# Aligned SBUF tiles, other buffer counts and a new order of the first batch's loads in a fused attention and mixer kernel

## The chip, the cores and the metric

The kernel runs on one core of a Trainium2 chip, in one launch. The metric is the time of an execution on the device in microseconds; a profiled execution also has a span, from the first to the last instruction that the profiler records. TensorE (PE) multiplies matrices, with its weight loads recorded apart (PEld); VectorE (DVE) and ScalarE (ACT) work elementwise, GpSimd (POOL) makes small copies and issues the loads from HBM, and SyncE (SP) issues the transposing DMAs and the stores. Each engine works through its own list of instructions in order.

## What is computed

Eight batches go through a gated attention without softmax and then through a mixer with two multilayer parts. Cut to what matters:

```python
batch, seq, d_model, d_qk = 8, 3008, 256, 64            # d_tok 256, d_ch 1536
scores = (1.0 / seq) * np.matmul(z, z.transpose(0, 2, 1))
attn   = np.maximum(scores, 0.0) ** 2
x      = u * np.matmul(attn, v)                          # the gate
h      = np.maximum(x.transpose(0, 2, 1) @ w_tok1, 0.0) @ w_tok2
y      = x + h.transpose(0, 2, 1)
out    = y + np.maximum(y @ w_ch1, 0.0) @ w_ch2          # float32
```

Queries and keys are the same z, so the scores are symmetric: the block of query block q and key block g is the transpose of the block of g and q.

## The kernel before

**Tiles.** The 3008 rows of a batch are cut into six blocks of 512 (the last has 448 rows, and its last 64 stand twice, in both halves of the partitions). A block of queries q meets six blocks of keys g. For each pair, one score-square tile `at` of 128 x 2048 bf16 is made: four score matmuls (line 379) with 64 rows of contraction, two at a time on the two halves of the array, write PSUM; ACT applies relu (417, or 405 on the diagonal); DVE squares in place (425, 453). Then eight matmuls (line 513, "av") multiply it with the tile of v, four for each half of the 256 columns, into the accumulators `acc0` and `acc1`. After six key blocks DVE multiplies the accumulators with the transposed u, `uT` (gate, line 606), and a transposing DMA on SP turns the result `xT` into `x_sb` (618). In this text six av blocks make a query block, and 36 av blocks, called steps, a batch.

**Mirrors.** Where symmetry is used, a tile `at` of block (q, g), g > q, is also turned by a transposing DMA on SP (`flip`, line 472) into a tile `fl`, the mirror, which serves block (g, q) later without scores, relu or square. Lines 224 to 227 say which blocks are made directly: all of batch 0, the upper half and the diagonal of each later batch, and in batch 1 also those with g = 0. On the diagonal of later batches only a triangle of scores is made and the rest is filled by transposes (465). Ten buffers hold mirrors, six hold `at`.

**Mixer.** When the last query block of a batch is done, its mixer is added to a list of pieces that PE runs between the av blocks of the next batch: `tok1` (653), `tok2` (670), `ch1` (707) and `ch2` (748). ch1's result `hp` is evacuated with relu by ACT (720) or DVE (722) into `h2` tiles (eight buffers); ch2's result `op` gets the residual on DVE (760, 775), and SP stores it (764, 778). Batch 7's mixer runs alone at the end.

**Order.** The order of every engine's instructions is written out beforehand by a planner in the kernel's own Python (lines 961 to 1045). It keeps clocks for PE, ACT, DVE and SP with due times for each kind of operation (`push(engine, ready, busy, lat, ...)`), and room counters (`live`, `ROOM`) for the buffers, and picks at each point a run of up to three pairs of scores, an av half or a mixer piece. Its times are constants; on the chip the engines wait for semaphores. Stretches of scores use half the array's rows, and PE's order changes between the two kinds of matmul 282 times.

**Loads.** `at_group(n, f)` (line 885) makes f be called when step n begins, so that its instructions go to the end of POOL's and SP's lists there. POOL's list is served in order: a load whose buffer is still in use, or a copy whose input has not landed, holds everything behind it. In batch 0 POOL carries the following. `load_v` of the batch's own six tiles at the start (line 149, from a pool of eight buffers that all batches share); `load_u` (160, two buffers; freed when `turn_u` has transposed the tile), two steps after each query block begins and two blocks ahead; w_tok1 (178), w_tok2 (189) and w_ch (208, 213) in turns from step 5 or 8 on; `order_w_tok2` (199, 203), which rewrites the loaded w_tok2 from its single staging buffer `ws` and so waits for that load; z of the next batch (99) from step 18 on, with a doubling copy for each (111) that waits for the load and for one of two buffers; and from step 28 on the six tiles of v of batch 1.

```python
at_group(base + (NQ - 1) * NG - 2 + (j if j > 1 else 0),
         lambda b=b, c=c: load_v(b + 1, c))
```

The lines that the change and the steps touch: 76 to 80 and 866 (constants and the small tile `mark`), 147, 158, 187 and 860 (pools of v, u, ws), 227, 270 (ROOM), 442, 614 and 701 (due times on SP), 735 to 783 (ch2 and its residual), 807 (needs of ch2), 901 to 907 and 930 to 942 (steps of the loads).

## Time and profile before

| what | value |
|---|---|
| 13 runs, median (lowest to highest) | 1175.47 us (1172.24 to 1186.24) |
| the profiled execution's own time | 1179.05 us |
| its span | 1177.2 us |
| mean granted TensorE clock | 0.998 |
| DVE, ACT, POOL busy | 47%, 44%, 14% of the span |
| HBM read, written | 65.40 MB, 24.64 MB: 76 GB/s |
| DMA packets | 462339, of them 426224 under 512 B |

The profiled execution took 3.58 us longer than the median of the runs, and 1.85 us of its time lie outside of the span. PE is busy nearly throughout, so the time is read from where PE is not busy or runs slowly, and from the number of its matmuls. A matmul record is longer than its turn on PE, since matmuls overlap; the pace is read from a run of them: 12 matmuls of 512 columns take 2.59 us on the chain that ended last, 0.216 us each. In the timeline, the bracket behind a row gives the idle time of the engine before it and what ended it.

### The profile page before, as it was taken

The numbers are of one execution on the slowest core, as the hardware profiler recorded it, in microseconds if no ns is written. First come the engines' busy times: TensorE is split into PE (matmuls) and PEld (weight loads), VectorE is DVE, ScalarE is ACT, GpSimd is POOL, SyncE is SP. The second block draws the span as 40 slices with busy tenths as digits, with TensorE's granted clock in tenths as the row PEclk, the third lists the DMA queues.
The fourth block names the chain that finished last, engine by engine and source line by source line (L and its number), as shares of the span: only waits on it lengthen the run. The fifth ranks groups of instructions, "written<-read, shape, count | busy, mean of one in ns | idle before, by whom it ended". The sixth has DMA issues, their size and how long they took to land.

```text
span 1177.2 us, 17741 instructions
## 1 busy us (share of the span) xinstructions
PE 1157.2 (98%) x6971; PEld 630.8 (54%) x7069; DVE 556.8 (47%) x836; ACT 523.5 (44%) x652; POOL 161.8 (14%) x328
## 2 busy tenths in 40 slices
PE   8998999999999999999999999999999999999998
PEld 3334455555546555465555655556455564555666
DVE  5774755445433554335534356342653337411544
ACT  7886544425533355433544345243553434433221
POOL 2372200101111010110201101012010110000000
PEclk9999999999999999999999999999999999999999
DMA  8999956998779987887959888699778989651232
GB/s 146 135 133 167 162 113 128 167 152 146 141 139 168 159 148 131 157 161 142 157 118 182 152 161 142 119 179 161 133 136 145 182 133 165 116 124 37 58 77 68
DMA packets 462339, 162.95 MB, mean 138 GB/s; under 512 B 426224, under 2 KB 439856, under 8 KB 462256
## 3 DMA queue, kind: packets, MB, share of 16 engines
q1 hardware_dynamic: 434400, 129.12, 60.1%
q0 software_dynamic: 27344, 32.32, 19.7%
q8 instruction: 55, 0.90, 0.3%
q10 hardware_dynamic: 512, 0.38, 0.1%
q14 instruction: 28, 0.23, 0.1%
HBM read 65.40 MB, written 24.64 MB: 76 GB/s over the span
## 4 chain that ended last, share of the span: by engine, by line
PE 90%; DMA 6%; POOL 2%; issue 1%; DVE 1%; ACT 0%; SPq 0%; POOLq 0%; DVEq 0%
PE acc L513 36%; PE op L748 21%; PE hp L707 21%; PE sc L379 5%; PE a_ps L653 4%; PE h_ps L670 3%; DMA ws<-in_moe_w_tok_dram 2%; DMA zT<-zr 1%; DMA ur<-in_u_dram 1%; DMA v_sb<-in_v_dram 1%; DMA uT<-ur 1%; POOL w_tok_sb L199 1%; DMA zf<-in_z_dram 1%; POOL v_sb L149 0%; POOL zr L111 0%
## 5 line engine op out<-in xcount | busy, mean ns | idle before, releaser
L417 ACT ACTIVATE at<-sc 128x1024 bf16<-128x1024 f32 (+1 forms) x294 | 281.0, 1023 | 212.2 <-PE sc L379 207.6
L513 PE MATMUL acc<-at,v_sb 128*128 128x512 bf16 (+2 forms) x1471 | 355.7, 379 | 8.9 <-DMA v_sb<-in_v_dram 5.7
L513 PEld LDWEIGHTS <-v_sb 128*128 128x128 bf16 (+1 forms) x2304 | 209.6, 98 | 275.4 <-issue 67.6
L720 ACT ACTIVATE h2pre<-hp 128x1024 bf16<-128x1024 f32 (+1 forms) x183 | 183.5, 1007 | 303.0 <-PE hp L707 300.3
L425 DVE TENSOR_TENSOR at<-at 128x1024 bf16<-128x1024 bf16 (+1 forms) x294 | 205.1, 705 | 178.2 <-ACT at L417 177.0
L707 PE MATMUL hp<-xT,w_ch_sb 128*128 128x512 bf16 (+1 forms) x1120 | 262.9, 374 | 1.6
L748 PE MATMUL op<-w_ch_sb,h2pre 128*128 128x256 bf16 x2208 | 258.4, 273 | 0.4 <-DVE xT L676 0.2
L748 PEld LDWEIGHTS <-h2pre 128*128 128x128 bf16 x2208 | 215.9, 98 | 46.2 <-issue 0.5
L513 PE MATMUL acc<-fl,v_sb 128*128 128x512 bf16 (+1 forms) x775 | 186.8, 370 | 1.9 <-issue 0.8
L707 PEld LDWEIGHTS <-w_ch_sb 128*128 128x128 bf16 x1152 | 112.7, 98 | 126.7
L760 DVE TENSOR_TENSOR res<-op,u_sb 128x512 f32<-128x512 f32 x88 | 60.9, 692 | 209.2 <-PE op L748 206.1
L722 DVE TENSOR_SCALAR h2pre<-hp 128x1024 bf16<-128x1024 f32 (+1 forms) x105 | 126.6, 1206 | 54.4 <-PE hp L707 53.3
L606 DVE TENSOR_TENSOR xT<-acc,uT 128x512 bf16<-128x512 f32 (+1 forms) x96 | 63.3, 665 | 109.0 <-PE acc L513 108.7
L405 ACT ACTIVATE at<-sc 128x512 bf16<-128x512 f32 (+3 forms) x164 | 59.3, 447 | 87.5 <-PE sc L379 75.8
L379 PE MATMUL sc<-zT 64*128 64x512 bf16 (+1 forms) x752 | 97.8, 360 | 0.3
L453 DVE TENSOR_TENSOR at<-at 128x512 bf16<-128x512 bf16 (+3 forms) x164 | 46.8, 338 | 47.9 <-ACT at L405 47.9
L111 POOL COPY zr<-zs 128x512 bf16<-128x512 bf16 x42 | 27.1, 646 | 294.0 <-DMA zT<-zr 293.5
L379 PEld LDWEIGHTS <-zT 64*128 64x128 bf16 x752 | 32.0, 94 | 57.8 <-issue 40.0
L160 POOL DMA_DIRECT2D ur<-in_u_dram x48 | 25.9, 541 | 236.6 <-DMA uT<-ur 234.4
L676 DVE TENSOR_TENSOR xT<-xT,h_ps 128x1024 bf16<-128x1024 bf16 (+1 forms) x48 | 55.6, 1192 | 5.5 <-PE h_ps L670 5.5
L670 PE MATMUL h_ps<-w_tok_sb,a_sb 128*128 128x512 bf16 (+1 forms) x184 | 43.9, 374 | 0.5
L149 POOL DMA_DIRECT2D v_sb<-in_v_dram x48 | 26.0, 546 | 134.1 <-PE acc L513 133.9
(43 smaller groups left out, 229.3 us busy)
## 6 DMA issues: line engine op xcount, KB each, us to landing
out_dram<-res SPq DMA_DIRECT2D x88, 256.0 KB, 2.4
v_sb<-in_v_dram POOLq DMA_DIRECT2D x40, 256.0 KB, 5.3
ur<-in_u_dram POOLq DMA_DIRECT2D x40, 256.0 KB, 5.5
zs<-in_z_dram POOLq DMA_DIRECT2D x35, 64.0 KB, 4.6
at<-at SPq DMA_TRANSPOSE x123, 2.6
fl<-at SPq DMA_TRANSPOSE x100, 4.5
v_sb<-in_v_dram POOLq DMA_DIRECT2D x8, 192.0 KB, 6.7
w_ch_sb<-in_moe_w_ch_dram POOLq DMA_DIRECT2D x4, 384.0 KB, 7.1
```

Of the source, the lines that this page charges most:

```text
L379: nc.tensor.matmul(sc[:, r, c0:c1], zT[h, k * P:(k + 1) * P], zT[h, q * QW + c0:q * QW + c1], start=True, stop=True)
L405: nc.scalar.activation(a3[:, i, c0:c1], sc[:, r, c0:c1], ACT.Relu, scale=inv_S)
L417: nc.scalar.activation(view, sv, ACT.Relu, scale=inv_S)
L425: nc.vector.tensor_mul(view, view, view)
L513: nc.tensor.matmul(o, vs[blk.b, g][rows, i, dh * P:(dh + 1) * P], rhs, start=first, stop=stop, skip_group_check=True)
L606: nc.vector.tensor_mul(xT[:, dh, :full * P].rearrange("p (t s) -> p t s", s=P), acc[:, :full * P].rearrange("p (t s) -> p t s", s=P), uT[: ...
L670: nc.tensor.matmul(h[:, dh, :W], st["a"][:, th, dh * P:(dh + 1) * P], w_tok2_sb[:, th, q * QW:q * QW + W], start=(th == 0), stop=(th == 1))
L707: nc.tensor.matmul(hp[:, r, :W], w_ch1_sb[:, dc, cc * P:(cc + 1) * P], xT[:, dc, :W], start=(dc == 0), stop=(dc == DT - 1))
L720: nc.scalar.activation(h2[:, :, :W], hp[:, :, :W], ACT.Relu)
L722: nc.vector.tensor_single_scalar(h2[:, :, :W], hp[:, :, :W], 0.0, AX.max)
L748: nc.tensor.matmul(op[:, i, :], h2, w_ch2_sb[:, cc, :], start=(cc == 0 and i == 0), stop=(cc == CHT - 1), skip_group_check=True)
L760: nc.vector.tensor_add(res.rearrange("p i (h d) -> p i h d", d=P), op.rearrange("p i (h d) -> p i h d", d=P), us[:, :, half * 2:half * 2 + ...
```

## The change

1. `mark` has 32 floats (128 bytes) and is the first constant; the tiles of the large pools then start on multiples of 256 bytes. In the built programs the first `at` tile starts at byte 118944 of a partition before (160 past a multiple of 256) and at 135424 after (a multiple).
2. `at` has seven buffers instead of six, `fl` eight instead of ten, `ur` three instead of two, `us` three instead of two. w_tok2 is staged in `h2` buffers (up to eight at a time) instead of the single `ws`, and so is the tile of zeros.
3. v of batch 0 lies in six of the eight mirror buffers; the `v` pool's eight are free for batch 1.
4. In batch 1 the blocks with g = 0 are no longer made directly: five mirrors take their place.
5. The loads of batch 0 come in one row, spread over steps 8 to 33: v of batch 1, w_tok1, w_tok2, w_ch. A staged w_tok2 tile is reordered four steps after its load is asked for. For batches from 2 on, z is loaded six steps sooner.
6. The planner's due times of SP's transposes are 7.5 and 8.0 us instead of 5.5 and 6.5; a ch2 piece may be placed by 0.218 us per pair of h2 sooner; the two pieces of the very last ch2 half use a PSUM tile each, so that each has its own residual and store.

```diff
+class Sooner:
+    def __init__(self, done, us):
+        self.done, self.us = done, us
+
+    @property
+    def t(self):
+        return None if self.done.t is None else self.done.t - self.us
...
+    mark = consts.tile([P, 32], F32)
     w_tok1_sb = consts.tile([P, KT, d_tok], BF16)
...
     def load_v(b, c):
-        vt = sb.tile([P, GK, D], BF16, tag="v", name="v_sb", bufs=8)
+        if b == 0:
+
+            vt = sb.tile([P, GK, D], BF16, tag="fl", name="v_sb", bufs=ROOM["fl"])
+            live["fl"] += 1
+        else:
+            vt = sb.tile([P, GK, D], BF16, tag="v", name="v_sb", bufs=8)
...
-        ur = sb.tile([P, QW // P, D], BF16, tag="ur", name="ur", bufs=2)
+        ur = sb.tile([P, QW // P, D], BF16, tag="ur", name="ur", bufs=3)
...
-        st = sb.tile([P, DT, QW], BF16, tag="ws", name="ws", bufs=1)
+        st = sb.tile([P, DT, QW], BF16, tag="h2", name="ws", bufs=ROOM["h2"])
...
-        return b == 0 or g >= q or (b == 1 and g == 0)
+        return b == 0 or g >= q
...
-    ROOM = {"at": 6, "fl": 10, "xT": 9, "x": 7, "h2": 8, "us": 2}
+    ROOM = {"at": 7, "fl": 8, "xT": 9, "x": 7, "h2": 8, "us": 3}
...
-            done = push("sp", t, 2.45, 6.5, lambda t: flip(b, q, g, at, uses, done),
+            done = push("sp", t, 2.45, 8.0, lambda t: flip(b, q, g, at, uses, done),
...
+            if blk.b == 0 and blk.q == NQ - 1:
+                live["fl"] -= 1
...
-            push("sp", t, 1.25, 5.5, lambda t: turn_x(b, q, t), first=1)
+            push("sp", t, 1.25, 7.5, lambda t: turn_x(b, q, t), first=1)
...
-                st["turned", q] = push("sp", u_done[q].t, 1.25, 5.5, lambda t: turn_u2(q))
+                st["turned", q] = push("sp", u_done[q].t, 1.25, 8.0, lambda t: turn_u2(q))
...
         def ch2(q, half, i, end):
-            if i == 0:
+            apart = alone(q, half)
+            if i == 0 or apart:
                 take_slot()
                 st["op"] = psum.tile([P, 2, D], F32, tag="ps", name="op", bufs=3)
...
+            over = i == pieces_of(q, half) - 1 and half == halves(q)[1]
+            if over:
+                live["h2"] -= CHT // 2
+            if i < pieces_of(q, half) - 1 and not apart:
                 return
...
-                if half * 2 + 1 < n:
+                if not apart and half * 2 + 1 < n:
                     nc.vector.tensor_add(
...
-                    ends = [(0, slice(0, P), us[:, :, k, :], rows_of(out[b], q)[:, k, :])]
-                    if i == 1:
+                    j = i if apart else 0
+                    ends = [(j, slice(0, P), us[:, :, k + j, :],
+                             rows_of(out[b], q)[:, k + j, :])]
+                    if both:
...
+        def alone(q, half):
+
+            return pieces_of(q, half) == 1 or (b, q, half) == (B - 1, NQ - 1, 0)
+
         def add_ch2(q, half, i):
-            two = pieces_of(q, half) == 2
-            tails.append(Piece(1.312, [h2_done[q, c2] for c2 in range(CHT // 2)] + w_done[2:],
+            two = not alone(q, half)
+            needs = [Sooner(h2_done[q, c2], 0.218 * c2) for c2 in range(CHT // 2)]
+            tails.append(Piece(1.312, needs + w_done[2:],
...
-    mark = consts.tile([P, 1], F32)
-    nc.gpsimd.tensor_copy(mark[:], zf0[NG - 2][:, 0, :1])
+    nc.gpsimd.tensor_copy(mark[:, :1], zf0[NG - 2][:, 0, :1])
...
-            at_group(base + 3 * NG, lambda b=b: new_zT(b + 1))
+            at_group(base + 2 * NG, lambda b=b: new_zT(b + 1))
+
+            first = base + (2 if b else 3) * NG
             for j, c in enumerate(vorder):
-                at_group(base + 3 * NG + j, lambda b=b, c=c, h=held: ask_z(b, c, h))
-                at_group(base + 3 * NG + j + 3, lambda b=b, c=c, h=held:
+                at_group(first + j, lambda b=b, c=c, h=held: ask_z(b, c, h))
+                at_group(first + j + 3, lambda b=b, c=c, h=held:
                          turn_next_z(b, c, h.pop(c)))
-                at_group(base + (NQ - 1) * NG - 2 + (j if j > 1 else 0),
-                         lambda b=b, c=c: load_v(b + 1, c))
+                if b:
+                    at_group(base + (NQ - 1) * NG - 2 + (j if j > 1 else 0),
+                             lambda b=b, c=c: load_v(b + 1, c))
...
-    for c in range(NG):
-        at_group(NG - 1 + 4 * c, lambda c=c: load_w_tok1(c))
-        at_group(NG + 1 + 4 * c, lambda c=c: load_w_tok2(c))
-        at_group(NG + 4 + 4 * c, lambda c=c: order_w_tok2(c))
...
-    for part in range(4):
-        n = NG + 2 + 6 * part
-        at_group(n, lambda part=part: ask_w_ch(part))
+    items = [lambda c=c: load_v(1, c) for c in vorder]
+    items += [lambda c=c: load_w_tok1(c) for c in range(NG)]
+    first_tok2 = len(items)
+    items += [lambda c=c: load_w_tok2(c) for c in range(NG)]
+    items += [lambda part=part: ask_w_ch(part) for part in range(4)]
+    for k, item in enumerate(items):
+        n = NG + 2 + k * (NQ * NG - 2 * NG + 2) // len(items)
+        at_group(n, item)
+        if 0 <= k - first_tok2 < NG:
+            at_group(n + 4, lambda c=k - first_tok2: order_w_tok2(c))
```

In the built programs PE has 7069 matmuls before and 7049 after (752 and 732 of them scores), in 141 and 134 stretches of half-array work; the flips are 100 and 105, ACT's relus on whole score pairs (line 417) 294 and 284, DVE's squares of them as many. The first 507 matmuls, into the first query block of batch 1, stand in the same order in both.

## Prediction

> **What bounds the kernel.** I read the page's first part, then the busy time by stretches, then who ended PE's waits, then the timeline where PE waits. The page:
>
> ```profile
> span 1177.2 us, 17741 instructions
> PE 1157.2 (98%) x6971; PEld 630.8 (54%) x7069; DVE 556.8 (47%) x836; ACT 523.5 (44%) x652; POOL 161.8 (14%) x328
> ```
>
> PE is busy for 98% of the span and nobody else for half of it, so an edit counts only if it takes matmuls away, ends a wait of PE, or shortens what follows the last matmul. The stretches (span, then PE, PEld, DVE, ACT, POOL busy, granted clock, DMA share, GB/s):
>
> ```profile
> 13.00:92.00 79.00, 77.75 (x418) 30.26 (x424) 56.59 (x82) 65.27 (x71) 34.66 (x55) 1.00 1.14 140
> 92.00:97.00 5.00, 2.60 (x14) 0.95 (x13) 4.77 (x9) 3.50 (x4) 2.70 (x4) 1.00 1.23 167
> 97.00:100.50 3.50, 1.62 (x12) 0.48 (x11) 1.02 (x2) 2.30 (x3) 2.21 (x5) 1.00 1.27 108
> 100.50:104.50 4.00, 4.00 (x11) 1.39 (x11) 1.05 (x2) 0.55 (x1) 0.53 (x1) 0.57 1.18 221
> 110.00:1105.00 995.00, 989.00 (x5979) 545.78 (x6062) 449.05 (x690) 421.21 (x544) 113.33 (x240) 1.00 0.81 142
> ```
>
> From 110 to 1105 us PE idles 6 us in 995. Nearly half of 92 to 100.5 us is idle, and just after it the clock is 0.57. PE's waits name the cause (total, times, longest), and PE's timeline shows the place, the start of batch 1:
>
> ```profile
> PE acc L513 <- DMA v_sb<-in_v_dram: 5.7, 3, 2.4
> PE acc L513 <- issue: 2.2, 14, 0.2
> ...
> 95.71 2.24 PE L513 MATMUL acc<-at,v_sb 128*128 128x512 bf16 x9 [2.35 <-DMA v_sb<-in_v_dram]
> 97.77 0.82 PE L379 MATMUL sc<-zT 64*128 64x512 bf16 x6
> 100.47 4.24 PE L513 MATMUL acc<-at,v_sb 128*128 128x512 bf16 x11 [1.88 <-DMA v_sb<-in_v_dram]
> ```
>
> POOL's timeline shows why v is late:
>
> ```profile
> 86.28 0.71 POOL L189 DMA_DIRECT2D ws<-in_moe_w_tok_dram  x1
> 86.98 1.14 POOL L149 DMA_DIRECT2D v_sb<-in_v_dram  x2
> ...
> 94.30 1.92 POOL L199 COPY w_tok_sb<-ws 128x384 bf16<-128x384 bf16 x2 [4.57 <-DMA ws<-in_moe_w_tok_dram]
> 96.17 0.75 POOL L203 COPY w_tok_sb<-ws 128x128 bf16<-128x128 bf16 x1
> 96.87 0.54 POOL L149 DMA_DIRECT2D v_sb<-in_v_dram  x1
> ```
>
> The first load of v(1) leaves at 86.98 us, and three leave only behind a copy that waited 4.57 us for w_tok2.
>
> **The change, part by part.**
>
> *Fewer scores (edit 4).* Five blocks lose four score matmuls each. Two run side by side, so ten pairs go. A matmul of 512 columns has a pace of 0.216 us: 10 x 0.216 = 2.16 us. Each stretch of scores also costs two changes of array mode: from the last full matmul before six scores to the first one after them the trace's starts lie 1.065 us apart, in all 36 such places, where four turns of 0.216 make 0.864; 0.10 us a change. Seven stretches fewer: 14 x 0.10 = 1.4 us. This is on the path: **-3.6 us**. The ten relus of 1.02 us and ten squares of 0.7 us that go too lie beside PE and count nothing. The five added flips (line 472) cost SP some 2.45 us each, around the start of batch 1, where SP issued for 3.6 us between 96 and 110 us. They cost PE nothing if x_sb, which shares SP, is in time (first rival). Five mirrors must be ready for use: relu 1.02, square 0.7 and the flip's landing of 4.5 us (its row among the DMA issues) make 6.3 us. Counting PE's order at 0.216 us a matmul, the nearest use of any mirror comes 26.9 us after its scores (21.4 before), and in later batches 44 us (38).
>
> *v of batch 1 early (edits 3 and 5).* With buffers of their own these loads wait for no matmul. On POOL they stand behind u of query block 3, whose buffer is free when uT of block 0 has landed, at 22.6 us in this trace. So the nine DMAs (some 0.55 us each) leave between 23 and 28 us; the longest landing of v in this stretch was 11.3 us, so all is there by about 40 us, against a need at 93.4. That takes away 2.35 + 1.88 us of idling and the slow clock: 4.0 us at 0.57 cost 4.0 x 0.43 = 1.72. Together **-5.95 us**.
>
> The Trainium skill ("TensorE: Matmul & The Clock Gate", Part 1: The HAM clock gate) has the clock halved after at least one idle window of about 3.4 us. Here neither idle time reaches that, and the clock fell all the same, so I go by the row. By the rule nothing of 1.72 would be the stall's, and the sum below would be smaller by that.
>
> What is late next there? The squares: of batch 1's second key block they end at 95.2 us in the trace, and PE, 2.35 us sooner, wants them at 96.3 (eight av, two tails and six scores after 93.4). So nothing to about 0.5 us is given back; I take 0.1 with the rounding.
>
> *What loads v(1) pass.* They now precede w_tok1, w_tok2 and w_ch. tok1 starts at 109.5 us in the trace, 103.5 after the gain; from step 22 to the end of batch 0 POOL has six loads of 0.7, thirteen reorders of about 0.85, four loads of w_ch of 0.7, four other loads of 0.55 and six copies of 0.6 to 1.07 us, about 25 us in 14 steps of 2.6. Eight staging buffers take away the wait of a load for the reorder ahead of it. I cost it at nothing; without that cover each reorder that waits holds POOL like the 4.57 us above.
>
> *ur, us, at buffers, z sooner, later due times (edits 2, 5, 6).* They remove POOL's wait for uT and alter the planner's order. PE has no wait on them in the trace, so they can gain only where PE idles now: 1.25 us from 13 to 92. From 110 on, adding up all matmuls at their paces and changes leaves about 4 us unexplained. Bounds: -4 us, if all such small waits go; +3, if the new order makes three quarters as many more. Nearest is the unchanged row, since the smallest distance from scores to use (1.8 us) and from scores to the reuse of their PSUM tile (1.15 before, 1.01 after) hardly move. I take 0.
>
> *Alignment (edit 1).* The trace has no aligned tile. PE waits for no transpose, and with 6.3 us needed of 26.9 a faster one reaches nobody, so it is worth 0; a gain or loss in the engines' reads is bounded by the same -4 and +3.
>
> The Trainium skill ("DMA: Bandwidth & Descriptors", How a descriptor splits into AXI transactions) says that a descriptor which starts off a multiple of 256 bytes fetches unused bytes as well. So these 256-byte rows should move in fewer beats; the sum stays the same by the rule and by the row, as PE doesn't wait there.
>
> *The end (edit 6).* The last residual and store now:
>
> ```profile
> 1172.56 0.69 DVE L760 TENSOR_TENSOR res<-op,u_sb 128x512 f32<-128x512 f32 x1 [1.41 <-PE op L748]
> ...
> 1173.28 0.34 SPq L764 DMA_DIRECT2D out_dram<-res  x1
> ```
>
> Half of it will be left: 0.42 us, as line 775 takes for 128x256, and a store of half the bytes (2.4 us for both sizes in the issues). That is 0.3 us, up to 0.6; **-0.4**. Against it, the order places a ch2 1.09 us behind its ch1 twice near the end instead of once (that once idled 0.08 + 0.27 us), and reuses one PSUM tile after 0.76 us, where a relu alone takes 0.92: **+0.6** (0 to 1).
>
> **Sum.** -3.6 - 5.95 + 0.1 - 0.4 + 0.6 = -9.25 us against the profiled 1179.05: 1169.8. That execution is 3.58 us above the median of the runs. I don't know that the median run has the whole slow clock, which depends on where the idling falls, so I count half of 1.72 there: 1175.47 - 9.25 + 0.86 = **1167.1 us**.
>
> **Rivals.**
>
> *The wait moves to x_sb, or to something else at the same place.* tok1's last eight matmuls need x_sb of the last query block. SP is through with the x_sb before it at 95.9 us; one added flip (2.45) now comes first, so it leaves at 98.4 and lands 4.3 us later, at 102.7, against a need at 103.5 + 4.4 = 107.9. Once it lands later than that, PE idles instead of gaining, and all of 5.95 can go. For it: transposes took up to 19 us to land in batch 0's crowded DMA (DMA share 1.14). Against it: v(1) is gone from that stretch. It gives 1175.47 - 3.6 - 0.4 + 0.6 = 1172.1 us, within 0.5%.
>
> *Slower: eight mirror buffers are too few.* After query block 1, nine flips have been made and eight are still needed; block 2 adds three and frees two only as it runs. A flip that finds no buffer keeps its `at`, one of seven, and SP or the planner's order stands. If PE then runs out of ready blocks, it waits a whole chain: scores 0.4, two relus of 1.02, square 0.7, 3.1 us; in seven batches 22 us. It gives 1167.1 + 22 = 1189; the kernel gets slower as a whole once a batch loses over 8.4 / 7 = 1.2 us. Against it: mixer pieces fill PE in every batch, and the mirrors' distances grew.
>
> *More than forecast.* The small waits go as well: 1167.1 - 4 = 1163.
>
> **How the numbers follow.** Forecast 0.68, x_sb or the like 0.20, too few mirrors 0.07, more 0.05. The forecast alone runs from 1164 to 1170. The range, 1162.5 to 1173.0 us, takes in the first rival and most of the last and leaves out the slower one and some stray tails. 0.5% (about what a measurement of this kernel can tell from no change) is 5.9 us: faster is below 1169.6. Forecast less its upper edge and "more" make 0.70 faster, the first rival with that edge 0.22 the same, 0.08 slower.
>
> **What would show it.** Right: v(1) issued before 30 us; no wait of PE on v near batch 1's start, no clock below 1 there; tok1 starting near 103.5 us; 134 stretches of scores; a last residual of 0.42 us; shorter landings of flips with PE no faster per matmul. Wrong: a new PE wait between 90 and 110 us on x_sb, a square or a mirror; idling per 100 us from 200 to 1000 above today's 0.6; another pace of the same matmuls.

## The result, and the profile after

The changed kernel takes 1187.41 us (median of 11 runs, 1177.13 to 1191.1), the kernel before 1173.63 us (48 runs): a ratio of **1.0089** (95% interval 1.0064 to 1.0114). It is slower, where 1167.1 us was forecast and the range ended at 1173.0. Ratios here follow the means of the runs (1185.73 and 1175.28 us) rather than the medians, whose quotient is 1.0117, since single runs of a kernel lie several us apart. The profiled execution took 1184.0 us. Its page, and the same stretches as before (span, then PE, PEld, DVE, ACT, POOL busy, granted clock, DMA share, GB/s), with two later ones added:

```profile
span 1182.2 us, 17701 instructions
PE 1156.5 (98%) x6958; PEld 631.0 (53%) x7049; DVE 540.4 (46%) x818; ACT 524.8 (44%) x651; POOL 160.2 (14%) x328
```
```profile
92.00:97.00 5.00, 4.95 (x30) 1.87 (x29) 4.40 (x10) 4.73 (x6) 1.05 (x2) 1.00 1.37 202
97.00:100.50 3.50, 3.50 (x21) 1.40 (x20) 2.20 (x4) 3.12 (x4) 0.00 (x0) 1.00 1.24 196
100.50:104.50 4.00, 4.00 (x24) 1.70 (x22) 2.11 (x6) 3.27 (x7) 1.01 (x2) 1.00 1.32 210
...
110.00:130.00 20.00, 15.10 (x76) 5.97 (x74) 11.33 (x15) 7.24 (x10) 0.00 (x0) 1.00 1.03 213
200.00:1105.00 905.00, 895.04 (x5411) 495.60 (x5479) 385.11 (x600) 378.03 (x481) 100.30 (x215) 1.00 0.77 143
```

The stall at 92 to 100.5 us is gone and the clock is 1.00 there, as forecast. But between 110 and 130 us PE idles 4.9 us, and from 200 to 1105 us 10.0, where it was 5.3 before (both traces lack about 1% of the matmul records, which count as idle here). Who ended PE's and ACT's waits (total, times, longest):

```profile
ACT at L437 <- DMA fl<-at: 15.7, 5, 7.8
PE hp L729 <- ACT at L437: 5.2, 2, 3.9
PE sc L399 <- ACT at L437: 3.0, 1, 3.0
PE acc L533 <- DVE xT L628: 2.2, 3, 1.9
```

The first line is the one to read. A relu writes an `at` tile, and it waits for a flip that still *reads* that tile (output `fl`, input `at`): the flip has kept its `at`, and PE, which wants ACT to empty its PSUM, waits behind ACT. The worst place, in the timelines of PE, ACT and SP's queue:

```profile
483.55 1.89 PE L729 MATMUL hp<-xT,w_ch_sb 128*128 128x512 bf16 x8
489.30 1.87 PE L729 MATMUL hp<-xT,w_ch_sb 128*128 128x512 bf16 x4 [3.86 <-ACT at L437]
```
```profile
488.23 1.02 ACT L437 ACTIVATE at<-sc 128x1024 bf16<-128x1024 f32 x1 [3.93 <-DMA fl<-at]
```
```profile
479.33 5.00 SPq L485 DMA_TRANSPOSE at<-at  x4
484.42 1.64 SPq L492 DMA_TRANSPOSE fl<-at  x1
```

SP issues four other transposes first, the flip leaves at 484.42, and the relu starts at 488.23. By then the clock has fallen: the four matmuls after the idle time take 1.87 us, where four of this kind take 1.02 at 634.67 us.

```profile
489.30:492.00 2.70, 2.70 (x7) 0.99 (x7) 1.47 (x2) 0.86 (x1) 0.00 (x0) 0.50 1.16 256
492.00:495.00 3.00, 3.00 (x12) 1.26 (x10) 0.43 (x1) 0.32 (x1) 0.00 (x0) 0.57 0.90 203
```

That is 2.70 x 0.50 + 3.00 x 0.43 = 2.6 us more. The stall at the start of batch 1 is of the same kind (SP's queue, ACT, PE):

```profile
104.14 12.04 SPq L492 DMA_TRANSPOSE fl<-at  x4
112.72 1.02 ACT L437 ACTIVATE at<-sc 128x1024 bf16<-128x1024 f32 x1 [7.80 <-DMA fl<-at]
...
113.79 0.88 PE L399 MATMUL sc<-zT 64*128 64x512 bf16 x4 [3.03 <-ACT at L437]
```

Four flips, made for the mirrors that the change adds, occupy SP for 12 us, and the relu waits for the first of them. Two waits on a diagonal's transposes follow them (1.00 at 120.31 and 0.72 at 121.65 us). The third loss lies in batch 0 (POOL, DVE, PE):

```profile
77.49 0.63 DVE L445 TENSOR_TENSOR at<-at 128x896 bf16<-128x896 bf16 x1 [0.99 <-ACT at L437]
...
78.23 2.38 POOL L220 COPY w_tok_sb<-ws 128x512 bf16<-128x512 bf16 x4
78.30 3.21 DVE L445 TENSOR_TENSOR at<-at 128x896 bf16<-128x896 bf16 x1 [0.18 <-ACT at L437]
...
82.17 2.05 PE L533 MATMUL acc<-at,v_sb 128*128 128x448 bf16 x10 [1.92 <-DVE xT L628]
```

One square takes 3.21 us instead of 0.63: it starts just behind POOL's first copy and ends after its fourth, and the gate behind it is late for PE.

The kernel before with aligned tiles and nothing else (e3 below, span 1170.5 us) is a fair "typical before": from it the profiled execution differs by +11.7 us. PE's list of matmuls (each at its pace, with 0.10 us for each change of array mode, as in the prediction) is 3.5 us shorter; the waits are 1.92 + (3.03 + 1.00 + 0.72) + 3.86 + 1.3 (the second of the hp waits, near 635 us), and the slow clock 2.6: 14.4 in all. That makes +10.9, and 0.8 us stay unassigned.

### The profile page after: what moved, and what is told of

Same layout as the page of the kernel before. It is cut to its first block, busy times and chain, and to the rows that moved or that the text cites. A ratio compares the mean times of both kernels' runs of the same rounds, so it can differ in the third digit from the quotient of the medians.

```text
span 1182.2 us, 17701 instructions
## 1 busy us (share of the span) xinstructions
PE 1156.5 (98%) x6958; PEld 631.0 (53%) x7049; DVE 540.4 (46%) x818; ACT 524.8 (44%) x651; POOL 160.2 (14%) x328
## 4 chain that ended last, share of the span: by engine, by line
PE 93%; DMA 2%; issue 2%; ACT 1%; DVE 1%; SPq 0%; POOL 0%; ACTq 0%; DVEq 0%
PE acc L533 40%; PE op L771 21%; PE hp L729 20%; PE sc L399 6%; PE a_ps L675 3%; PE h_ps L692 3%; DMA fl<-at 1%; ACT at L437 1%; DMA zf<-in_z_dram 0%; DVE xT L698 0%; DMA v_sb<-in_v_dram 0%; DVE xT L628 0%; DVE at L445 0%; DMA at<-at 0%; DVE h2pre L744 0%
## 5 line engine op out<-in xcount | busy, mean ns | idle before, releaser
L437 ACT ACTIVATE at<-sc 128x1024 bf16<-128x1024 f32 (+1 forms) x284 | 271.5, 1021 | 252.2 <-PE sc L399 235.6
L533 PE MATMUL acc<-at,v_sb 128*128 128x512 bf16 (+2 forms) x1441 | 348.1, 378 | 5.9 <-DVE xT L628 1.9
L742 ACT ACTIVATE h2pre<-hp 128x1024 bf16<-128x1024 f32 (+1 forms) x192 | 192.2, 1004 | 316.8 <-PE hp L729 315.9
L445 DVE TENSOR_TENSOR at<-at 128x1024 bf16<-128x1024 bf16 (+1 forms) x284 | 201.0, 713 | 213.9 <-ACT at L437 213.4
L729 PE MATMUL hp<-xT,w_ch_sb 128*128 128x512 bf16 (+1 forms) x1121 | 268.6, 376 | 7.3 <-ACT at L437 5.2
L533 PE MATMUL acc<-fl,v_sb 128*128 128x512 bf16 (+1 forms) x811 | 201.2, 372 | 1.9 <-DVE xT L628 0.3
L744 DVE TENSOR_SCALAR h2pre<-hp 128x1024 bf16<-128x1024 f32 (+1 forms) x96 | 115.8, 1206 | 48.7 <-PE hp L729 46.0
L675 PE MATMUL a_ps<-x_sb,w_tok_sb 128*128 128x256 bf16 x384 | 45.5, 273 | 0.0
```

The costliest lines, as they stand in the source:

```text
L437: nc.scalar.activation(view, sv, ACT.Relu, scale=inv_S)
L445: nc.vector.tensor_mul(view, view, view)
L533: nc.tensor.matmul(o, vs[blk.b, g][rows, i, dh * P:(dh + 1) * P], rhs, start=first, stop=stop, skip_group_check=True)
L675: nc.tensor.matmul(st["a_ps"][:, th, :], w_tok1_sb[:, k, th * P:(th + 1) * P], x[:, :, i, :], start=(k == 0 and th == 0), stop=(k == KT - ...
L729: nc.tensor.matmul(hp[:, r, :W], w_ch1_sb[:, dc, cc * P:(cc + 1) * P], xT[:, dc, :W], start=(dc == 0), stop=(dc == DT - 1))
L742: nc.scalar.activation(h2[:, :, :W], hp[:, :, :W], ACT.Relu)
```

## The experiments

In each group the kernel named is compared with the kernel before on the same chip. Theories: **M**, eight mirrors are too few; **Z**, the sooner z; **S**, the five added flips; **P**, POOL's reorder copies; **A**, alignment; **D**, the due times.

### First round: one part undone

**e1, ten mirrors again** (the changed kernel, four counts back):

```diff
-    ROOM = {"at": 7, "fl": 8, "xT": 9, "x": 7, "h2": 8, "us": 3}
+    ROOM = {"at": 6, "fl": 10, "xT": 9, "x": 7, "h2": 8, "us": 2}
-        ur = sb.tile(..., bufs=3)
+        ur = sb.tile(..., bufs=2)
```

> The changed kernel with the buffer counts of before (ten mirrors, six score squares, two u, two us); all else as changed. The planner puts off 34 of 105 flips for want of a mirror buffer here, against 67 of 105 in the changed kernel and 23 of 100 before. Theory M (too few mirrors: a put-off flip keeps its score square, relu waits for that buffer, PE for relu's PSUM tile): the waits of relu on a flip in batches 3 and 4 (3.9 and 1.4 us of PE in the changed kernel's profile, and 2.3 us of slow clock) go, the time falls by 6 us or more below the changed kernel's, to 1170 to 1180. Rival theory A (alignment slows the engines or DMAs) and theory S (the five added flips at batch 1's start hold SP): no change in batches 3 and 4, time within 3 us of the changed kernel's.

1186.29 us, 1.0117 (1.0101 to 1.0132). M's gain did not come: ACT waits on flips 19.6 us in five places, PE 3.7 us on a mirror at 111 us. Ten mirrors alone cure nothing.

**e2, old rule for direct blocks** (the changed kernel):

```diff
-        return b == 0 or g >= q
+        return b == 0 or g >= q or (b == 1 and g == 0)
```

> The changed kernel, with the blocks of batch 1 with g = 0 made directly again, so without the five added mirrors. Theory S: relu's wait of 7.8 us at batch 1's start goes, and with it 3.2 + 1.2 + 0.8 us of PE's waiting between 113 and 122 us; twenty more score matmuls cost 2.7 us by PE's list; net 2 to 3 us faster than the changed kernel. The planner still puts off 61 of 100 flips, so theory M expects the waits in batches 3 to 7 to stay and the time to stay well above the kernel before.

1188.74 us, 1.0136 (1.0109 to 1.0162). The stall at 113 us is gone, as S says; a new one of 8.9 us on x_sb at 406 us and four waits of hp on ACT (7.7 us) replace it. S is right of the place and is not the whole.

**e3, alignment alone** (on the kernel before):

```diff
+    mark = consts.tile([P, 32], F32)
     w_tok1_sb = consts.tile([P, KT, d_tok], BF16)
...
-    mark = consts.tile([P, 1], F32)
-    nc.gpsimd.tensor_copy(mark[:], zf0[NG - 2][:, 0, :1])
+    nc.gpsimd.tensor_copy(mark[:, :1], zf0[NG - 2][:, 0, :1])
```

> The kernel before with the alignment alone (mark of 128 bytes as the first constant); every engine's list is the same as before. Theory A: slower than before by several us, with PE's pace or waits changed. Theories M, S and P: no slower, at most a little faster, since aligned tiles make transposes land sooner (flips 3.9 us against 4.5 in the two profiles) and PE waits for few of them: -3 to 0 us against before.

1172.36 us, 0.9983 (0.9966 to 0.9999). A falls as a cause. Its trace shows something else, at the stretch that carried the forecast (stretches, POOL's timeline, PE's wait):

```profile
92.00:97.00 5.00, 4.95 (x28) 1.87 (x27) 4.18 (x10) 4.73 (x6) 0.00 (x0) 1.00 1.12 210
97.00:100.50 3.50, 3.50 (x20) 1.35 (x19) 2.34 (x4) 3.12 (x4) 0.23 (x1) 1.00 1.05 155
```
```profile
78.83 1.15 POOL L150 DMA_DIRECT2D v_sb<-in_v_dram  x2
...
85.51 1.43 POOL L200 COPY w_tok_sb<-ws 128x384 bf16<-128x384 bf16 x2 [2.58 <-DMA ws<-in_moe_w_tok_dram]
```
```profile
PE acc L514 <- DMA v_sb<-in_v_dram: 0.5, 2, 0.3
```

With the order of the kernel before, the first v of batch 1 leaves at 78.83 us, not at 86.98, and PE hardly waits for v. The five other traces with these old loads (e7, e10, e13, e14, e18), four of them unaligned, show the same: first v between 72.9 and 79.6 us, at most 1.0 us of waits on v, no slow clock at 92 to 104.5. So the stall that the forecast was built on is not what the kernel usually does. The profile before has one slow load ahead of v on POOL:

```profile
59.45 1.69 POOL L199 COPY w_tok_sb<-ws 128x512 bf16<-128x512 bf16 x2 [12.98 <-DMA ws<-in_moe_w_tok_dram]
```

POOL waited 12.98 us for this part of w_tok2; in the six other traces the same wait is 4.22 to 5.68 us. That difference is as large as the 8 us by which v left later.

**e4, no reorder copies** (the changed kernel; the columns of w_tok2 are not reordered, so this part of the computation is left out):

```diff
         nc.gpsimd.dma_start(
-            out=st[:, :, :W],
+            out=w_tok2_sb[:, :, c * QW:c * QW + W],
...
     def order_w_tok2(c):
-        st = ws.pop(c)
...
+        return
```

> The changed kernel without POOL's reordering copies of w_tok2: the loads go straight into their place, so the columns of w_tok2 stand in the order of memory and not of the rows (part of the computation is changed). Theory P (four and more copies in a row on POOL hold up a square on DVE, 3.21 us instead of 0.63 at 78.3 us, and with it the gate): the wait of 1.9 us of PE at 80.2 us goes, about 2 us faster than the changed kernel; rest unchanged. If DVE's long square has another cause, the wait stays.

1183.35 us, 1.0087 (1.0067 to 1.0107). The wait of 1.92 us near 80 us goes and no square there takes over 0.73 us, so P names its cause; the other stalls stay. The ratio, against 1.0089, is too coarse to show the 2 us.

### Second round: z and the due times

**e5, old z steps** (the changed kernel):

```diff
-            at_group(base + 2 * NG, lambda b=b: new_zT(b + 1))
+            at_group(base + 3 * NG, lambda b=b: new_zT(b + 1))
-            first = base + (2 if b else 3) * NG
+            first = base + 3 * NG
```

> The changed kernel with z of the next batch asked for at the old step (18 for every batch). Theory Z (z six steps sooner ends POOL's waits for zT early, so u and the first tiles of v leave POOL in one burst about 25 us sooner, in the middle of the batch, and the flip that SP issues behind them takes 5 to 10 us instead of 1.6): v's first loads move back behind zT's last transposes, the waits of PE behind relu in batches 2 to 7 go, PE idles about 0.6 us per 100 us from 200 to 1100, the time falls by 6 to 10 us below the changed kernel's, to 1177 to 1181; the stall at batch 1's start stays. Theory M (eight mirrors; 45 of 105 flips put off here): within 3 us of the changed kernel.

1201.26 us, 1.0246 (1.0218 to 1.0274). Missed: it got worse. PE now waits on the mirrors themselves in five places, in the middle of the batches:

```profile
PE acc L533 <- DMA fl<-at: 21.3, 5, 6.6
```

**e6**, the edits of e5 and e2 together:

> The changed kernel with the old step of z and with the blocks of g = 0 of batch 1 made directly again. Theories Z and S together: no stall in batches 2 to 7 and none behind the five mirrors at batch 1's start; PE's list is 3.1 us longer than with z alone put back (1154.5 against 1151.4), the stall of 5 us goes, so 1 to 4 us faster than that kernel, 1173 to 1178. If the stall at batch 1's start is not of the five mirrors but of loads queued ahead of uT there, it stays and this kernel is 2 to 3 us slower than with z alone put back.

1184.7 us, 1.0104 (1.0083 to 1.0124): missed as well. Nothing waits at batch 1's start, but PE still waits 5.5 us on two mirrors, at 349 and 641 us.

**e7**, the kernel before with only the sooner z (e5's edit the other way round):

> The kernel before with z six steps sooner from batch 1 on, and nothing else of the change. Theory Z by itself: PE waits behind relu in some of the batches 2 to 7 as in the changed kernel, 1177 to 1184. If the third u buffer is needed for the burst as well (POOL still waits there for uT with two), no change: 1171 to 1175.

1179.91 us, 1.0058 (1.0035 to 1.008): the sooner z costs by itself, with ten mirrors; PE waits 2.9 us for ACT near 619 us, which waits for a flip that still reads its `at`.

**e8, old due times** (the changed kernel):

```diff
-            done = push("sp", t, 2.45, 8.0, lambda t: flip(b, q, g, at, uses, done),
+            done = push("sp", t, 2.45, 6.5, lambda t: flip(b, q, g, at, uses, done),
-            push("sp", t, 1.25, 7.5, lambda t: turn_x(b, q, t), first=1)
+            push("sp", t, 1.25, 5.5, lambda t: turn_x(b, q, t), first=1)
-                st["turned", q] = push("sp", u_done[q].t, 1.25, 8.0, lambda t: turn_u2(q))
+                st["turned", q] = push("sp", u_done[q].t, 1.25, 5.5, lambda t: turn_u2(q))
```

> The changed kernel with the planner's due times of before (6.5 and 5.5 us). The number of flips put off is the same (67 of 105). If later due times cause the stalls (the planner counts on score squares at other moments), the time falls to 1180 or less; theories Z and M: within 3 us of the changed kernel.

1196.91 us, 1.0191 (1.0164 to 1.0217): the later due times are a gain where mirrors are scarce. ACT's waits on flips double, to 31.6 us.

So the edits don't add. Undoing one of several causes leaves or worsens the loss, and each must be seen from the kernel before as well.

### Third round: pairs, and single parts on the kernel before

**e9, ten mirrors and old z** (e1's edit and e5's):

> The changed kernel with both ten mirror buffers (and six at, two ur, two us) and the loads and transposes of the next z back at their old steps. Everything else of the change stays: the five added flips, the new loads, alignment, later due times, the new end. Theory M and Z together (in batches 2 to 7 eight mirrors and the sooner z each hold `at` tiles or mirrors up, and either alone is enough to keep the loss; ten mirrors with sooner z gave 1.0117, eight with old z 1.0246): the stalls after 200 us go, the one of some 3 to 5 us at the start of batch 1 (five added flips) and the 2 us near 80 us (reorders) stay, so 1174 to 1178 us, 1.001 to 1.005. Rival D, the later due times or the new end are what costs: stalls after 200 us stay, 1183 or more. Rival S alone (the five flips cost in every batch): the same as D, with the waits on mirrors used by the first query blocks.

1178.06 us, 1.0025 (1.0006 to 1.0044): M and Z together hold, and D falls. After 200 us PE has no wait of 0.5 us or more; what is left lies at the start of batch 1, where it was said (ACT, PE):

```profile
108.13 2.86 ACT L437 ACTIVATE at<-sc 128x1024 bf16<-128x1024 f32 x3 [7.60 <-DMA fl<-at]
```
```profile
108.08 1.62 PE L533 MATMUL acc<-fl,v_sb 128*128 128x512 bf16 x4 [2.86 <-DMA fl<-at]
```

**e10, the four counts alone** on the kernel before:

```diff
-    ROOM = {"at": 6, "fl": 10, "xT": 9, "x": 7, "h2": 8, "us": 2}
+    ROOM = {"at": 7, "fl": 8, "xT": 9, "x": 7, "h2": 8, "us": 3}
-        ur = sb.tile(..., bufs=2)
+        ur = sb.tile(..., bufs=3)
```

> The kernel before with one edit: eight mirror buffers, seven at, three ur and three us in place of ten, six, two and two. Nothing else is changed. Theory M (eight mirrors are too few): PE waits on a mirror or on ACT behind an `at` that a late flip holds, in several batches, 3 us each: 1178 to 1190 us, 1.005 to 1.015. Rival Z (only the sooner z, whose loads and transposes then meet u's and v's, costs): within 0.3% of before, 1169 to 1176, since the other counts give it a little.

1215.2 us, 1.0353 (1.0313 to 1.0392). Larger than M had said, and the opposite of the rival.

**e12** is the changed kernel with the edits of e1, e2, e5 and e8, so that alignment, the new loads and the new end are left of the change. **e11** also takes back the end:

```diff
-            return pieces_of(q, half) == 1 or (b, q, half) == (B - 1, NQ - 1, 0)
+            return pieces_of(q, half) == 1
-            needs = [Sooner(h2_done[q, c2], 0.218 * c2) for c2 in range(CHT // 2)]
+            needs = [Sooner(h2_done[q, c2], 0.0 * c2) for c2 in range(CHT // 2)]
```

> The kernel before with alignment and the new loads alone: v of batch 0 in mirror buffers, v of batch 1 loaded from 24 us on, then w_tok1, w_tok2 (staged in h2 buffers) and w_ch. Ten mirrors, six at, two ur and us, old z steps, old rule for direct blocks, old due times and old end. By the reading that v of batch 1 cost a typical run little (alignment alone left one wait of 0.5 us on it), the new loads gain at most 1 us and lose the 2 us of the reorders that meet the squares near 80 us: 1171 to 1175, 0.998 to 1.002. By my forecast's term of 5.95 us for v it would be 1166 to 1168.

1174.3 us, 0.9996 (0.9976 to 1.0016): v early is worth nothing that can be measured.

> As the kernel with alignment and the new loads alone, with the new end added (the last query block's residual in two halves, ch2 placed sooner). My forecast's terms for the end (-0.4 and +0.6 us) and for the scores that this order saves (the list of matmuls is 2.3 us shorter) give 0 to 2.5 us less than that kernel. Rival: ch2 placed so soon after ch1 idles PE each time, so that the saving is given back: the same or up to 2 us more, with PE waits on relus in ch2.

1174.95 us, 0.9996 (0.9979 to 1.0013): the new end neither gains nor loses. (The shorter list in its expectation was a miscount: both have 141 stretches of scores and 1155.7 us of matmuls.) Near 80 us two squares take 4.42 us beside the copies and PE waits 2.3 us.

### Fourth round: how many mirrors

**e13, eight mirrors, nothing else** (on the kernel before):

```diff
-    ROOM = {"at": 6, "fl": 10, "xT": 9, "x": 7, "h2": 8, "us": 2}
+    ROOM = {"at": 6, "fl": 8, "xT": 9, "x": 7, "h2": 8, "us": 2}
```

> The kernel before with eight mirror buffers in place of ten and nothing else changed: six at, two ur, two us, old z, old due times, old loads. The planner puts off 37 of 100 flips for want of a mirror (23 before). Theory M (the mirrors alone are the cause of what all four counts together cost, 1.0353): PE waits on mirrors of 5 to 7 us in several batches, 1195 to 1220 us, 1.02 to 1.04. Rival: the seventh at and the third ur and us set the planner on an order that reuses things too soon, and mirrors are only one part: below 1.01, at most 1185.

1207.48 us, 1.0291 (1.0262 to 1.0319): 34 us for two buffers, against 41 us for all four counts, with intervals that overlap. On the kernel before the mirrors are the cause; the three other counts were not run by themselves. PE's waits, PE's worst place and SP's queue there:

```profile
PE acc L513 <- DMA fl<-at: 26.0, 4, 9.1
```
```profile
503.18 3.35 PE L513 MATMUL acc<-fl,v_sb 128*128 128x512 bf16 x8 [9.12 <-DMA fl<-at]
```
```profile
490.88 3.65 SPq L472 DMA_TRANSPOSE fl<-at  x1
494.62 4.72 SPq L112 DMA_TRANSPOSE zT<-zr  x1
```

The flip of 490.88 is held at the head of SP's queue until PE has read the last of an old mirror (494.08 by the semaphores), and lands at 503.14, just before PE can go on. From there to its landing are 9.06 us, twice the median of this run's flips (4.6); POOL's loads of v leave from 490.60 us on. Whether these loads make it slow, no run separates.

**e14, alignment and the new end** (e12 with the loads of the kernel before):

> The kernel before with alignment and the new end alone (last residual in halves, ch2 placed sooner): old loads, old counts, old z, old rule, old due times. My forecast had -0.4 and +0.6 us for the end. Against before: alignment's 0.9983 and about 0, so 1171 to 1173.5, 0.997 to 1.0. If ch2 placed sooner idles PE each time, 1174 or more with waits of PE on relus in ch2.

1173.24 us, 0.9999 (0.9983 to 1.0016).

**e15, e12 with the reorder copies spread** over the steps:

```diff
-            at_group(n + 4, lambda c=k - first_tok2: order_w_tok2(c))
+            for h in range(DT):
+                at_group(n + 3 + 2 * h, lambda c=k - first_tok2, h=h: order_w_tok2(c, h))
```

> The kernel with alignment, new loads and new end, in which the copies that reorder w_tok2 are spread: one copy of a half at a step and two steps between, in place of two at one step. Theory P (a square that meets a run of POOL's copies is held until the run ends: 4.42 us for two squares where 1.26 is usual): with no runs of copies the wait of 2.3 us on xT near 80 us goes, 1 to 2.5 us less than that kernel, below 1173. Rival: each single copy holds a square about as long as its share, so the same time, with the wait cut in pieces.

1174.73 us, 1.001 (0.9997 to 1.0023). PE's wait near 80 us shrinks to 0.8 us, but POOL, held up by its other waits, still runs four copies in a row at 80.66 us, and the time is no shorter.

**e16, the changed kernel with ten mirrors, old z and the old rule** (e9 and e2's edit):

> The changed kernel with ten mirrors, old z steps and the old rule for direct blocks, so the loads, alignment, the later due times and the new end are what is left of the change. It differs from the kernel at 1.0025 only in that batch 1's first blocks need no flips. Theory S (the five added flips cost 3 to 5 us at the start of batch 1 even where mirrors are in plenty): 1173 to 1175, 0.998 to 1.001, and no wait of ACT behind a flip near 112 us. Rival D (the later due times cost with ten mirrors): stays at 1177 to 1179.

1173.74 us, 0.9998 (0.9984 to 1.0012): against e9 the five flips cost 0.27%, 3 us, and with them all that the change had lost is back. The two intervals overlap a little, but the traces agree: e9 has waits of 2.86 + 1.14 us and 3.42 us at half the clock at the start of batch 1, and e16 has neither, against a list that is 2.6 us shorter in e9: 4.0 + 1.7 - 2.6 = 3.1 us. From 200 to 1105 us PE idles 0.9 us (this trace lacks no matmul record, so about half of the difference to the changed kernel's 10.0 is made by the records lost there), and no wait of ACT or PE on a flip is left:

```profile
200.00:1105.00 905.00, 904.09 (x5514) 497.37 (x5513) 397.84 (x611) 374.74 (x481) 103.58 (x222) 1.00 0.76 143
```

### Fifth round: nine and eleven

**e17**, e16 with `"fl": 11` and `bufs=7` for v; **e18**, the kernel before with `"fl": 9`, as e13 otherwise:

> The kernel with the new loads, alignment, new end and later due times, old z and old rule (1173.74 us with ten mirrors), now with eleven mirror buffers; one v buffer of eight is given up for it (v of batch 0 takes mirror buffers, so eight are rarely all in use). The planner puts off 12 of 100 flips in place of 24. Theory M with plenty at ten: PE has no wait on a mirror any more with ten, so an eleventh buffer gains nothing: 1172.5 to 1175, within 0.2% of it. Rival: the small loss spread over the batches comes from put-off flips too: 1169 to 1171.

1173.52 us, 0.9989 (0.9965 to 1.0013): ten are plenty.

> The kernel before with nine mirror buffers and nothing else changed. The planner puts off 30 of 100 flips (23 with ten, 37 with eight). Theory M as a threshold in the planner's order: a flip that is put off past its use costs PE a chain of 5 to 9 us wherever it happens, so nine costs about half of what eight does or less: 1178 to 1192. Rival: any lack costs the same, 1203 or more; or nine are enough, below 1175.

1194.89 us, 1.0181 (1.0133 to 1.0229), a little above what was expected: no cliff at one number. The flips put off are counted in the planner's own run: those that are due but find `live["fl"]` at its limit.

| mirrors, rest of the kernel before | 8 | 9 | 10 |
|---|---|---|---|
| ratio | 1.0291 | 1.0181 | 1 |
| flips that the planner puts off for want of a mirror, of 100 | 37 | 30 | 23 |
| PE's list of matmuls, us | 1154.3 | 1154.9 | 1155.7 |

| with loads, alignment, end and later due times of the change | 10 mirrors | 8 mirrors (and `at` 7, `ur` 3, `us` 3) |
|---|---|---|
| old z, old rule | 0.9998 (e16) | 1.0104 (e6) |
| old z, five more flips | 1.0025 (e9) | 1.0246 (e5) |
| sooner z, old rule | not run | 1.0136 (e2) |
| sooner z, five more flips | 1.0117 (e1) | 1.0089 (the change; 67 of 105 put off) |

No version beats the kernel before by more than e3's 0.17%, whose interval ends at 0.9999.

## Why the prediction was wrong

**The step that failed is the price of the buffers.** The sum has no term for two mirrors fewer and takes 0 for the sooner z. Alone on the kernel before these cost 34 us (e13) and 0.58%, 7 us (e7); in the changed kernel the loss goes when the four counts and z are taken back (e9), and to the last part the five added flips (e16). Beside that, the largest gain in the sum, 5.95 us, was to come from a stall that six of seven traces with the old loads don't have. The sign that was named for being wrong came too: PE's idling from 200 to 1105 us went from 5.3 to 10.0 us.

**"Fewer scores, -3.6 us": right in size, and bought.** 134 stretches and a list that is 3.5 us shorter, as worked out. But in the table every loss of a mirror also shortens the list: with eight mirrors alone the built program has 134 stretches too (e13), and with ten mirrors, old z and the five added flips 139 (e9). So the 1.4 us for seven stretches were not edit 4's. A shorter list is no sign of a shorter time.

**"v of batch 1 early, -5.95 us": right in place, wrong as a term.** The loads left between 23.98 and 28.48 us, nothing waits for v at batch 1's start, the clock stays at 1.00. But a typical execution of the kernel before does not have that stall (e3 and five other traces), and alignment with the new loads measures 0.9996 (e11). The working saw that the profiled execution stood 3.58 us above the median and took off 0.86 for it; the whole term belonged to that execution, whose span is 6.7 us longer than e3's. Without it the forecast would have been some 5 us later, inside "no change" but still not slower.

**"ur, us, at buffers, z sooner, later due times: I take 0, bounds -4 and +3": failed in both directions.** Sooner z alone costs 0.58% (e7); the later due times are worth 1% with eight mirrors (1.0191 without them in e8, 1.0089 with them). The counts of `at`, ur and us were not run apart from the mirrors. "The smallest distance from scores to use hardly moves" was the wrong measure: PE's waits in the traces hang on the moment at which a flip *leaves* and lands.

**The rival "eight mirror buffers are too few": right, at 0.07.** Its chain (a flip without a buffer keeps its `at`) is the first wait of the profile after. That its price, 1189 us, lies near the 1187.41 measured is luck: it adds 3.1 us in each of seven batches to a forecast that held 5.95 us too much gain, while the profile has 4.75 us of waits at batch 1's start and then 3.86 and 1.35 us in two places. What spoke against it failed: the mixer pieces don't cover it, since ch1 itself waits, behind ACT, for the `at`; and longer distances from scores to use did not help.

A warning lay in the planner's own rules: flips put off for want of a mirror go from 23 of 100 to 67 of 105. It is no measure of the loss: e5 puts off 45 of 105 and loses 2.46%, the change 67 and loses 0.89%, and with the new z the loss stays at ten mirrors with 34 put off (e1). Why the sooner z costs with ten mirrors and helps with eight (e5 against the change) is not settled: no run tells what the new place of z's transposes does on SP from what the planner's whole list becomes.

**"The added flips cost PE nothing if x_sb is in time": failed.** x_sb was in time. The flips cost by holding `at` (113.79 us above) and, in e9, by landing late themselves (108.08 us); e9 against e16 sizes them at 3 us.

**"What loads v(1) pass: at nothing": failed, by a wait of 1.92 us in this trace**, not by waiting loads but by copies that run in a row beside squares (e4). The time doesn't show it: e12 has such a wait of 2.32 us and measures 0.9996. But in e17's profiled execution the wait of 2.31 us there also brought 3.41 us at half the clock, and that execution took 1177.18 us where the median is 1173.52. The cover that I named, the staging buffers, is what lets the copies bunch.

**Alignment at 0 and the end at +0.2: right** within what can be measured (0.9983 with an interval that ends at 0.9999; e12 against e11, e14 against e3). The last residual takes 0.42 us, as forecast, where it took 0.69:

```profile
1177.54 0.42 DVE L801 TENSOR_TENSOR res<-op,u_sb 128x256 f32<-128x256 f32 x1 [0.89 <-PE op L771]
```

## What to carry to other kernels

A buffer count in a hand-planned order is not read from who waits today. Count how often the plan itself puts an operation off for want of that buffer, before and after, and ask which tile the operation that is put off keeps. A count that rises is a reason to try the buffers alone; here it did not tell the size of the loss. A stall seen in one profiled execution may not be there in others: this one was in none of six further traces. Where edits share a resource, try each from both ends: here undoing the main cause alone gained nothing.

## What the runs showed of the hardware

A square on DVE with both inputs in SBUF takes 0.63 us alone and 3.21 us beside four copies of POOL (in e12 one of them takes 3.48 us). The Trainium skill ("SBUF — State Buffer", Who interferes with whom) says that a DVE instruction with two SBUF inputs contends with a GpSimd instruction that reads SBUF; the trace agrees. But a run of copies doesn't always hold a square to its end. In e11 four copies and the five squares beside them alternate: a copy takes 1.05 us on average, and a square, after the first, 1.06 (POOL and DVE in the stretch 80.92 to 84.9):

```profile
80.91 4.05 POOL L220 COPY w_tok_sb<-ws 128x512 bf16<-128x512 bf16 x4
80.89 4.56 DVE L445 TENSOR_TENSOR at<-at 128x896 bf16<-128x896 bf16 x5
```

Three squares and two copies do so in the profile after, too, from 82.63 us on. What decides between the two was not tested.

Flips land in a median of 4.5 us before and 4.6 in e13, both unaligned, and in 3.9 (after, e16) and 3.8 (e3) when tiles start on multiples of 256 bytes. PE, which doesn't wait for them, gains next to nothing.

The length of one idle time doesn't decide when the clock falls: it fell after 2.35 and 1.88 us with work between them (before) and not after 3.03 us (after, 113.79 us). After a kernel's start the profiles show it at 0.50 for 3.41 us, or for twice or three times that (10.24 us in e2). The stretch of 3.41 us ahead of each fall, and the slow stretch itself (before, after, e9; columns as above):

```profile
97.32:100.73 3.41, 1.53 (x12) 0.49 (x11) 1.25 (x2) 2.53 (x3) 1.89 (x5) 1.00 1.28 101
100.73:104.14 3.41, 3.41 (x10) 1.21 (x9) 0.82 (x2) 0.32 (x1) 0.53 (x1) 0.50 1.16 222
484.35:487.76 3.41, 1.09 (x6) 0.39 (x4) 1.80 (x2) 0.00 (x0) 0.00 (x0) 1.00 0.80 195
487.76:494.59 6.83, 5.29 (x14) 1.87 (x13) 1.92 (x2) 1.94 (x2) 0.00 (x0) 0.50 1.02 234
104.98:108.39 3.41, 0.55 (x4) 0.20 (x3) 0.00 (x0) 0.26 (x1) 0.00 (x0) 1.00 1.22 227
108.39:111.81 3.42, 3.42 (x16) 1.59 (x16) 2.52 (x4) 2.60 (x3) 0.00 (x0) 0.50 1.11 248
```

PE was busy for 1.53, 1.09 and 0.55 us ahead of the falls. Falls lie on a grid: in e5 the clock falls at 113.63, 212.61, 355.97, 509.57, 652.93 and 939.65 us, which are 29, 42, 45, 42 and 84 times 3.413 us apart. On such a grid, counted back from the fall at 487.76 us, the idle time of 3.03 us in the profile after lies across two stretches with 1.88 and 1.82 us busy (108.88 to 115.71), and the clock stayed at 1.00. It also stayed there after 1.55 us (before, 93.90 to 97.31), so close to 1.53 that these traces give no threshold. The Trainium skill ("TensorE: Matmul & The Clock Gate", Part 1: The HAM clock gate) has the clock halved after at least one idle window of about 3.4 us. The length fits; but the clock fell after stretches of that length in which PE was not idle throughout, so here the measurement decides.
